# RWKV-6 linear attention and a star-ReLU MLP on one core: attention outputs transposed on TensorE to the end, one cumulative-sum product from chunk-batch 8, and a new hand-written order

## The chip, the cores and the metric

The program runs on one core of a Trainium2 chip. Its engines are TensorE (PE; its weight loads are a row of their own, PEld), VectorE (DVE), ScalarE (ACT), GpSimd (POOL) and SyncE (SP), which issues every DMA here. The metric is device microseconds of one execution, lower is better. An engine takes its instructions strictly in the order in which the program lists them, so an instruction that waits holds up everything behind it on its engine.

## The reference

Four batches, eight heads, 768 steps, 48 channels per head. The attention keeps a 48 x 48 state per head, and its output feeds an MLP with 3072 tokens, 384 inputs and 2048 hidden units.

```python
for t in range(S):
    cur = np.einsum('bhd,bhe->bhde', u[None] * kt, vt)
    y[:, :, t] = np.einsum('bhd,bhde->bhe', rt, state + cur)
    state = wt[:, :, :, None] * state + np.einsum('bhd,bhe->bhde', kt, vt)
...
x = np.ascontiguousarray(attn_out.transpose(0, 2, 1, 3)).reshape(B * S, H * D)
h = x @ w_in
r = np.maximum(h, 0.0)
g = s * (r * r) + b
return (g @ w_out).astype(np.float32)
```

## The kernel before

**Chunk-batches.** The 768 steps are cut into six chunks of 128, and with four batches this makes 24 chunk-batches, numbered n = 0 to 23. Chunk-batches 0 and 1 are two chunks of one batch that are handled as a packed pair; the last four (n = 20 to 23) need no new state. Two chunk-batches make one MLP tile T = 0 to 11 of 256 tokens.

**Attention steps of chunk-batch n**, with the names that the order uses:

- `load n.0` to `n.3` bring w, r, k, v (192 KB each; 384 KB for the pair 0 and 1). `ln` (ACT, line 316) takes log w.
- `cum` (PE) makes the cumulative sums over time: a strict one (line 386, tile `cums` half 0) and a negated inclusive one (line 390, half 1), one 128 x 384 product each, and four one-column products for the chunk's total decay (line 395). `exp` (ACT, lines 410 and 412) turns both halves, 768 columns, into factors `E`. `l2` (POOL) spreads the decay.
- The kernel has a second form of this, which is off: from chunk-batch `ONE` on, only the strict product is made and exponentiated, `inc` (DVE, line 422) adds log w to the strict sum in PSUM, and `exn` (ACT, line 432) takes the exponential of the negated sum. `ONE = 24` means never.
- `mul` (DVE, line 449) multiplies r and k by the factors. `tr` (PE) and `tev` (ACT) transpose the products for n below 9; from 9 on (`DTK`), `tev` is one DMA transpose (line 505).
- `mt` (PE, line 541) makes the 128 x 128 score tiles, `msk` (DVE, line 552) masks them, `dmm` (PE, line 636), `sup` (DVE) and `st` (POOL) update the state, `ymm` (PE, lines 595 and 604) makes the output, `rkp`, `rku`, `yd` (POOL) and `cd` (DVE) its u-term, `vb` the bf16 cast of v, and `yev` (DVE, line 649) the sum of both, `x_sb`.
- `x_sb` must be transposed for the MLP. For n below `DTX = 12`, `xtr` (PE, line 697) makes three 128 x 128 transposes into PSUM, and `xev` (ACT, line 712) copies them to `xT`. From 12 on, `xev` is a DMA transpose that SP issues (line 515), and there is no `xtr`.

**MLP steps of tile T.** `g1 T.i` (PE, line 746) makes hidden columns in eight parts of six 256-column products; `relu T.i` (ACT, line 759) evacuates each, 128 x 512, from PSUM; `sq T.i` squares it on ACT (line 769) or DVE (line 771). `g2 T.i` (PE, line 790) is the second product in parts of four 384-column products, `oev` (DVE, line 801) its evacuation, `store` the DMA out. `li`, `lo` load the two weights in four pieces of 768 KB, `ci`, `co` cast them. `g1` parts 0 and 1 need piece 0 of w_in, parts 2 and 3 piece 1, parts 4 and 5 piece 2, parts 6 and 7 piece 3.

**PSUM rings.** `cum` and `mt` share one buffer (ring A): each waits until the one before it has been evacuated. `tr`, `dmm`, `ymm` and `xtr` share two (ring B), `g1` has two (h), `g2` two (o).

**The order.** All of this is issued in one list written out by hand, `ORDER`. A word is a step; `@A`, `@D`, `@P` put it on ACT, DVE or POOL; `+5` means five idle 128 x 256 matmuls (line 1107) on PE. Without a suffix, a square goes to ACT where T is 2 or more and 8T + i is odd, otherwise to DVE. Where the order begins the first tile, before:

```
dmm0 mul2 +5 cum3
load4.0 exp3 sup0 +5 tr2 rkp3 st0 cd1 +1 mt1
```

Of the kernel before, what the change touches and what calls it, by code (L numbers as in the profile page):

```python
# [10 lines left out]
AF = mybir.ActivationFunctionType  # L11
# [12 lines left out]
VB = 6  # L24
PK = 2
PKD = 1.55
ONE = 24
DTK = 9
DTX = 12
DK2 = 24  # L30
DX2 = 24
SQE = 'DA'
# [3 lines left out]
SLACK = 0.2  # L36

ORDER = """
load0.0 load_u load0.2 load0.1 load2.0 load0.3 ln0 +15 u_mm ln1 load3.1 +1 cum0 exp0 load3.0 +5
cum1 l20 mul0 load2.1 exp1 rkp0 +1 tr0 load2.2 ln2 mul1 tev0 +6 cum2 load3.2 u_ev +2 tr1 exp2 rku0  # L40
li0 tev1 l21 cd0 rkp1 load3.3 vb1@A +14 mt0 vb0@A msk0 rku1 ln3 load2.3 +5 dmm0 mul2 +5 cum3
load4.0 exp3 sup0 +5 tr2 rkp3 st0 cd1 +1 mt1 tev2 yd0 msk1 li1 rkp2 ci0 li2 +13 ymm0 mul3 li3 mt2
l22 yev0 yd1 tr3 msk2 +1 ymm1 lo0 tev3 vb2 rku2 yev1 +2 xtr0 +1 mt3 xev0 rku3 xtr1 cd2 ln4 +1 dmm2
xev1 sup2 yd2 vb3@A cd3 +6 g10.0 ci1@A msk3 ymm2 l23 yd3 dmm3 g10.1 yev2 relu0.0 cum4 lo1 sup3
xtr2 relu0.1 g10.2 sq0.0 small2 sq0.1@A ci2@D dmm1 relu0.2 g10.3 load5.0 sup1 xev2 g10.4 sq0.2
relu0.3 ci3 ymm3 relu0.4 g10.5 yev3 load4.1 xtr3 relu0.5 g10.6 co0 xev3 g10.7 relu0.6 sq0.4
colsum0 load4.2 sq0.3@A g11.0 exp4 lo2 co1 g20.4 relu0.7 lo3 g20.0 l24 sq0.5 ln5 load4.3 colsum1
sq0.6 relu1.0 g20.5 sq0.7 g11.1 load6.0 g11.2 relu1.1 mul4 cum5 relu1.2 g11.3 rkp4 load5.1 exp5
g20.1 sq1.0@A co2 g11.4 relu1.3 tr4 sq1.1 relu1.4 load5.2 st3 g11.5 sq1.3@A colsum2 co3 relu1.5
load6.1 g20.2 tev4 g20.6 vb4 small rku4 colsum3 sq1.5@A mt4 cssplit load7.0 g20.7 msk4 l25 st1  # L50
csspread g20.3 load6.2 csevac sq1.2 dmm4 ln6 g11.6 mul5 load6.3 cum6 relu1.6 load5.3 rkp5 g11.7
oev0.1 exp6 load8.0 tr5 cd4 rku5 g21.4 oev0.0 ln7 load7.1 tev5 sup4 g21.5 yd4 st2 st4 ymm4 load7.2
relu1.7 mul6 cum7 g21.0 exp7 load7.3 rkp6 yev4 tr6 sq1.7@A mt5 load9.0 sq1.4 tev6 g21.1 l27 cd5
vb5 msk5 xtr4 ln8 rku6 load8.1 g21.2 xev4 dmm5 g21.6 vb6@A yd5 sup5 load8.2 sq1.6@A cum8 l26 ymm5
mul7 exp8 load9.1 dmm6 g21.3 rkp7 yev5 vb7@A g21.7 load10.1 sup6 xtr5 cd6 l28 mt6 rku7 xev5
load9.2 oev1.0 tr7 ln9 g12.0 msk6 tev7 st5 load8.3 g12.1 yd6 relu2.0 dmm7 cum9 load10.2 relu2.1
mul8 ymm6 exp9 g12.2 load10.0 rkp8 yev6 g12.3 relu2.2 sup7 mt7 load13.0 st6 relu2.3 tr8 msk7
sq2.2@A g12.4 rkp9 store0.0 tev8 g12.5 oev1.1 sq2.0@A ymm7 load11.0 sq2.1@D mt8 relu2.4 sq2.3@D
xtr6 cd7 g22.0 vb8@A load9.3 msk8 yd7 relu2.5 g12.6 ln10 load11.3 l29 g12.7 rku9 yev7 sq2.4@A
load12.0 g22.4 xev6 relu2.6 sq2.5@D dmm8 xtr7 st7 store0.1 relu2.7 g22.1 sup8 sq2.6@A cd9 rku8  # L60
g22.5 load10.3 xev7 cum10 ln11 mul9 g13.0 exp10 load11.1 g13.1 sq2.7 mul10 g22.2 load11.2 relu3.1
g22.6 tev9 l210 cd8 relu3.0 rkp10 ln12 ymm8 cum11 sq3.0@A yd9 g13.2 load13.1 exp11 yd8 g22.3 tev10
relu3.2 g13.3 rku10 oev2.0 cum12 relu3.3 load13.2 g13.4 sq3.2 vb9@A rkp11 yev8 g22.7 ln13 cd10
load12.1 sq3.1 g13.5 mul11 exp12 xtr8 dmm9 load12.2 oev2.1 g23.4 xev8 sup9 mt9 relu3.4 g23.0 st9
relu3.5 msk9 tev11 sq3.5 g13.6 st8 vb10@A g13.7 relu3.6 sq3.4 dmm10 l211 load12.3 ymm9 sq3.3 vb11
sup10 mt10 load13.3 rku11 relu3.7 yev9 g23.5 sq3.6@A msk10 xtr9 l212 store1.1 g23.1 rkp13 xev9
g23.6 sq3.7@D g14.0 yd10 load15.0 ymm10 relu4.0 mul12 dmm11 cum13 load14.0 g14.1 st10 yev10 exp13
cd11 g23.2 store1.0 rkp12 vb12@A xtr10 load14.1 mt11 relu4.1 g14.2 mul13 sq4.1 load14.2 sq4.0@A
g14.3 sup11 relu4.2 g23.3 msk11 st11 load14.3 sq4.2@A g14.4 tev12 yd11 ln14 g23.7 relu4.3 rku12
oev3.0 cum14 relu4.4 oev3.1 ymm11 load15.1 exp14 g14.5 l213 yev11 tev13 g14.6 sq4.3@D ln15 l214  # L70
relu4.5 sq4.4 cum15 rku13 xev10 load16.0 g14.7 exp15 mul14 xtr11 g24.4 relu4.6 load15.2 g24.0 l215
sq4.6@A sq4.5@D vb14 cd12 relu4.7 g24.5 load15.3 rkp14 xev11 dmm12 mt12 vb13@A g15.0 yd12 msk12
tev14 g15.1 relu5.0 g24.1 sup12 sq5.0@A sq4.7@D relu5.1 mt13 load17.0 ymm12 ln16 g15.2 yev12 dmm13
cd13 rkp15 g24.2 xev12 msk13 g15.3 yd13 store2.1 dmm14 g24.6 sup13 relu5.3 st12 store2.0 relu5.2
cum16 mul15 ymm13 sq5.1 load16.1 g24.3 exp16 rku15 sup14 g15.4 load16.2 vb15@A yev13 mt14 load18.0
rku14 relu5.4 cd15 g15.5 xev13 ln17 msk14 g24.7 sq5.3 st13 relu5.5 g15.6 load16.3 oev4.1 sq5.2@A
ymm14 cum17 tev15 dmm15 g25.4 exp17 mul16 g15.7 store3.1 l217 oev4.0 g25.5 load17.1 rkp16 ln18
cd14 sq5.5 g25.0 relu5.6 sq5.4 tev16 cum18 l216 sup15 relu5.7 yd14 g25.6 sq5.7 g16.0 st14 yev14
exp18 store3.0 g16.1 sq5.6 relu6.0 xev14 rku16 mt15 sq6.0@A g16.2 relu6.1 msk15 vb16 load17.2
g25.7 yd15 relu6.2 g16.3 st15 load19.0 ymm15 relu6.3 g25.1 load18.1 yev15 g16.4 sq6.3@D load17.3  # L80
oev5.1 g25.2 relu6.4 dmm16 xev15 sq6.2@A g16.5 sup16 sq6.1 g25.3 mul17 relu6.5 load18.2 mt16 rkp17
cd16 g26.0 ln19 tev17 msk16 g16.6 st16 g26.1 relu6.6 oev5.0 load19.1 cum19 sq6.6@A vb17 g26.4
store4.1 sq6.5 l218 yd16 sq6.4@A g26.5 load19.2 exp19 g17.0 rku17 g16.7 relu7.0 rkp18 load18.3
ymm16 relu6.7 g17.1 yev16 g17.2 store4.0 cd17 relu7.1 sq6.7@D xev16 mt17 mul18 relu7.2 dmm17 g26.2
sq7.1 sup17 load20.0 sq7.0@A g26.3 msk17 g17.3 rkp19 load20.1 g17.4 load19.3 oev6.0 yd17 ymm17
relu7.4 load20.2 g26.6 rku18 yev17 relu7.3 g26.7 tev18 sq7.2 g17.5 vb18 ln20 g27.0 sq7.4 l219
relu7.5 sq7.3@D xev17 g17.6 st17 oev6.1 sq7.5 g27.1 relu7.6 mul19 load21.0 dmm18 sq7.6@A cum20
g17.7 vb19 cd18 exp20 tev19 g27.4 rkp20 relu7.7 g27.5 sq7.7 mul20 load20.3 dmm19 g27.2 rku20 sup18
mt18 tev20 g18.0 msk18 rku19 g27.3 relu8.0 store5.1 sup19 yd18 g18.1 sq8.0@A cd19 load21.1 ymm18
cd20 relu8.1 yd19 g18.2 supn20 yev18 ln21 mt19 relu8.2 xev18 g18.3 msk19 yd20 g18.4 relu8.3  # L90
load21.2 g27.6 sq8.1@D relu8.4 store5.0 cum21 sq8.2@A ymm19 exp21 oev7.0 g18.5 load22.0 yev19
vb20@A g28.0 load23.0 sq8.3@D relu8.5 sq8.4 mt20 g18.6 sq8.5@D load22.1 msk20 g27.7 xev19 rkp21
g28.1 g28.2 load22.2 mul21 g18.7 ln22 load23.1 st19 oev7.1 ymm20 relu8.6 cum22 rku21 g28.4
load23.2 exp22 g28.5 st18 tev21 relu8.7 g28.6 ln23 sq8.7@D g19.0 sq8.6@A load21.3 g19.1 relu9.0
mul22 store6.0 cum23 relu9.1 g19.2 rkp22 yev20 exp23 tev22 g19.3 rku22 relu9.2 g28.7 relu9.3 g19.4
mul23 xev20 sq9.0@A g19.5 relu9.4 supn21 cd21 mt21 sq9.2@A store6.1 cd22 g19.6 sq9.1 load22.3
msk21 vb21 relu9.5 g28.3 rkp23 sq9.3 g19.7 oev8.0 relu9.6 tev23 yd21 ymm21 sq9.6@A g29.4 relu9.7
yev21 g29.5 sq9.5 sq9.4 mt22 xev21 g29.6 oev8.1 supn22 msk22 store8.0 g29.0 vb22@A yd22 load23.3
g29.1 sq9.7 rku23 ymm22 store7.0 g29.2 yev22 g29.3 store7.1 cd23 xev22 mt23 g110.0 msk23 g29.7
relu10.0 g110.1 supn23 vb23 g110.2 yd23 oev9.1 relu10.1 ymm23 store9.1 sq10.0 relu10.2 g110.3  # L100
sq10.1@D yev23 g110.4 relu10.3 oev9.0 xev23 g210.0 relu10.4 g210.4 sq10.4 store8.1 sq10.2 g110.5
sq10.3@D g110.6 relu10.5 g210.1 sq10.5@D relu10.6 g110.7 g210.2 relu10.7 g111.0 sq10.6@A g111.1
relu11.0 g210.5 sq11.0 relu11.1 sq10.7@D g111.2 g210.3 relu11.2 g111.3 oev10.0 g111.4 sq11.1@D
relu11.3 store10.0 store9.0 g211.0 sq11.3@D relu11.4 g111.5 sq11.4@A sq11.2@A g111.6 relu11.5
g210.6 relu11.6 g111.7 sq11.5 g210.7 relu11.7 g211.1 oev10.1 g211.2 sq11.7@D store10.1 sq11.6
g211.4 g211.8 g211.3 g211.5 oev11.0 g211.6 g211.9 store11.0 g211.7 g211.10 oev11.1 g211.11
store11.1 oev11.2 store11.2
"""

class Plan:  # L110

    def __init__(self, rings):
# [41 lines left out]
def kernel(  # L158
# [13 lines left out]
    nc = tc.nc  # L172

    B, H, S, D = r.shape
    L = 128
# [75 lines left out]
    xT = [None] * NT  # L251
# [455 lines left out]
    def xevac(n):  # L707
        c = cb[n]
        T, j = divmod(n, CPT)
        if j == 0:  # L710
            xT[T] = mlp.tile([128, KT, TOK], BF16, name="xT", tag="xT", bufs=XTB)
        nc.scalar.copy(out=xT[T][:, :, j * L : (j + 1) * L], in_=c["xt_ps"])


    def load_win(i):
# [21 lines left out]
    hs = {}  # L737
# [18 lines left out]

    def relu(T, i):
        rh = mlp.tile([128, FPQ, TOK], BF16, name="rh", tag="rh", bufs=4)
        nc.scalar.activation(out=rh, in_=hs[T, i], func=AF.Relu)  # L759
        hs[T, i] = rh  # L760

    def sq_eng(T, i):
# [385 lines left out]
```

## Time and profile before

| what | value |
|---|---|
| median of 13 runs | 191.34 us (188.84 to 192.5) |
| the profiled execution, time | 191.34 us |
| its span, first to last instruction | 189.5 us |
| outside the span | 1.84 us |
| PE busy | 182.7 us (96% of the span) |
| ACT busy | 134.3 us (71%) |
| DVE busy | 128.9 us (68%) |
| POOL busy | 104.6 us (55%) |
| granted TensorE clock | 1.00 |

Busy time counts an instruction from its start to its end. On PE a matmul overlaps the next one, so what a matmul costs in a dense stream is the distance from its start to the next start, not its duration: one `g1` part shows a duration of 0.82 us and the next one starts 0.65 us later. The same holds, less strongly, on DVE and ACT, where the end of one instruction overlaps the start of the next by about 0.1 us.

### The profile page before, as it was taken

To read this page: it belongs to the slowest core of one execution; us is meant where nothing else is said; L and a number is where in the kernel's file an instruction comes from. 1 tells how busy PE (TensorE), PEld (TensorE's weight loads), DVE (VectorE), ACT (ScalarE), POOL (GpSimd) and SP (SyncE) were. 2 spreads that over 40 slices of the span, in tenths; PEclk is the share of its full clock that TensorE was granted. 3 is DMA by queue.
4 is the path that set the end of the run, shared out by engine and by line. 5 is a ranking of instruction groups with operands and counts; after the bars stand their busy time and mean duration, and the time that the engine had idled before them with its cause. 6 is when DMAs were issued, how large, how long until landed. Compare 5 with 4: busy or idle time off the path is not lost.

```text
span 189.5 us, 5062 instructions
## 1 busy us (share of the span) xinstructions
PE 182.7 (96%) x1984; PEld 142.8 (75%) x1984; DVE 128.9 (68%) x214; ACT 134.3 (71%) x254; POOL 104.6 (55%) x138
## 2 busy tenths in 40 slices
PE   7999989999989999999999999999999999999992
PEld 5577868877659878877877877788787786788872
DVE  7368775757969964797959945478698668562241
ACT  3496696795969898959976896776685698157720
POOL 3667913227979659596558394837935575200000
PEclk9999999999999999999999999999999999999999
DMA  5999998998979899997997988889688897630212
GB/s 144 249 213 246 287 386 264 273 238 170 203 150 212 187 215 201 184 216 173 205 171 167 174 209 167 169 205 224 137 179 191 174 216 153 189 92 17 83 42 83
DMA packets 122601, 35.32 MB, mean 186 GB/s; under 512 B 117329, under 2 KB 120530, under 8 KB 122578
## 3 DMA queue, kind: packets, MB, share of 16 engines
q1 hardware_dynamic: 122578, 35.01, 82.3%
q8 instruction: 15, 0.25, 0.5%
q14 instruction: 8, 0.07, 0.1%
HBM read 25.17 MB, written 4.72 MB: 158 GB/s over the span
## 4 chain that ended last, share of the span: by engine, by line
PE 65%; SPq 17%; DMA 11%; issue 2%; ACT 1%; POOL 1%; DVE 1%; DVEq 0%; ACTq 0%
PE o_ps L790 27%; PE h_ps L746 27%; SPq L295 14%; DMA wi_st<-in_moe_w_in_dram 5%; DMA wt<-in_w_dram 3%; PE mt_ps L541 3%; DMA rkt<-in_k_dram 3%; PE y_ps L604 2%; PE y_ps L595 2%; SPq L303 1%; PE cums L386 1%; PE cums L390 1%; PE d_ps L636 1%; SPq L717 1%; POOL w_in L878 1%
## 5 line engine op out<-in xcount | busy, mean ns | idle before, releaser
L759 ACT ACTIVATE rh<-h_ps 128x512 bf16<-128x512 f32 x96 | 56.1, 597 | 28.3 <-PE h_ps L746 27.0
L746 PE MATMUL h_ps<-xT,w_in 128*128 128x256 bf16 x576 | 74.9, 273 | 0.9 <-ACT rh L759 0.6
L790 PE MATMUL o_ps<-w_out,gT 128*128 128x384 bf16 (+1 forms) x400 | 73.3, 320 | 0.0
L746 PEld LDWEIGHTS <-w_in 128*128 128x128 bf16 x576 | 60.8, 114 | 6.5 <-DVE w_in L880 0.9
L790 PEld LDWEIGHTS <-gT 128*128 128x128 bf16 x400 | 36.7, 98 | 16.7
L321 POOL TENSOR_TENSOR rkp<-rkt 128x384 f32<-128x384 f32 x22 | 27.3, 1242 | 16.8 <-DMA rkt<-in_k_dram 16.8
L769 ACT ACTIVATE gT<-rh 128x512 bf16<-128x512 bf16 x52 | 32.0, 628 | 0.5
L552 DVE TENSOR_TENSOR mt_sb<-mt_ps,tri_strict 128x1024 bf16<-128x1024 f32 x22 | 26.8, 1219 | 6.1 <-PE mt_ps L541 6.1
L449 DVE TENSOR_TENSOR prd<-rkt,E 128x768 bf16<-128x768 f32 x22 | 24.7, 1125 | 6.5 <-ACT E L410 3.5
L327 POOL TENSOR_TENSOR rku<-rkp,u_bc 128x384 f32<-128x384 f32 x24 | 25.6, 1072 | 2.1 <-DVE u_bc L903 1.8
L771 DVE TENSOR_TENSOR gT<-rh 128x512 bf16<-128x512 bf16 x44 | 20.2, 479 | 7.0 <-ACT rh L759 7.0
L410 ACT ACTIVATE E<-cums 128x768 f32<-128x768 f32 x24 | 19.5, 811 | 7.3 <-PE cums L378 2.8
L350 POOL TENSOR_TENSOR yd<-vt,cd 128x384 bf16<-128x384 f32 x22 | 18.3, 837 | 8.4 <-DVE cd L344 6.2
L801 DVE SCALAR_TENSOR_TENSOR o_sb<-o_ps,s_bc,bconst 128x384 f32<-128x384 f32 (+1 forms) x25 | 14.9, 597 | 11.4 <-PE o_ps L790 11.2
L649 DVE TENSOR_TENSOR x_sb<-y_ps,yd 128x384 bf16<-128x384 f32 x24 | 13.3, 553 | 11.6 <-PE y_ps L604 8.9
L686 POOL TENSOR_TENSOR st<-stmp,l 128x384 bf16<-128x384 bf16 x16 | 15.1, 947 | 3.8 <-DVE stmp L677 3.8
L1107 PE MATMUL warm_ps<-warm_sb 128*128 128x256 bf16 x84 | 13.6, 299 | 1.1 <-DVE warm_sb L1064 1.1
L316 ACT ACTIVATE logw<-wt 128x384 bf16<-128x384 f32 x22 | 11.6, 529 | 3.1 <-DMA wt<-in_w_dram 3.1
L344 DVE TENSOR_REDUCE cd<-rku 128x8 f32<-128x384 f32 x24 | 12.9, 542 | 1.2 <-POOL rku L327 1.2
L462 POOL TENSOR_TENSOR l<-E,par 128x8 f32<-128x8 f32 x20 | 6.8, 341 | 11.2 <-ACT E L412 11.2
L878 POOL CAST vb<-vt 128x384 bf16<-128x384 f32 x11 | 6.0, 544 | 11.2 <-DMA vt<-in_v_dram 7.2
L1107 PEld LDWEIGHTS <-warm_sb 128*128 128x128 bf16 x84 | 8.2, 106 | 3.4 <-DVE warm_sb L1064 1.0
(93 smaller groups left out, 176.6 us busy)
## 6 DMA issues: line engine op xcount, KB each, us to landing
out_dram<-o_sb SPq DMA_DIRECT2D x23, 192.0 KB, 2.4
wt<-in_w_dram SPq DMA_DIRECT2D x22, 192.0 KB, 4.2
rkt<-in_r_dram SPq DMA_DIRECT2D x22, 192.0 KB, 3.8
rkt<-in_k_dram SPq DMA_DIRECT2D x22, 192.0 KB, 3.8
vt<-in_v_dram SPq DMA_DIRECT2D x22, 192.0 KB, 3.6
wi_st<-in_moe_w_in_dram SPq DMA_DIRECT2D x4, 768.0 KB, 6.4
wo_st<-in_moe_w_out_dram SPq DMA_DIRECT2D x4, 768.0 KB, 7.8
pkt<-in_w_dram SPq DMA_DIRECT2D x1, 384.0 KB, 3.4
```

The lines of the kernel that those rows point to most:

```text
L295: nc.sync.dma_start(out=dst, in_=src[bb, :, t0 : t0 + L, :].transpose([1, 0, 2]))
L321: nc.gpsimd.tensor_tensor(out=rkp, in0=c["r"], in1=c["k"], op=ALU.mult)
L327: nc.gpsimd.tensor_tensor(out=rku.rearrange("t h d -> t (h d)"), in0=c["rkp"].rearrange("t h d -> t (h d)"), in1=u_bc, op=ALU.mult,)
L410: nc.scalar.activation(out=E[:, :, 0:HD], in_=ps[:, :, 0:HD], func=AF.Exp)
L449: nc.vector.tensor_tensor(out=prd[:, :, :, 0:D], in0=c["rk"], in1=c["E"][:, :, 0:HD].rearrange("t x (h d) -> t x h d", h=H), op=ALU.mult,)
L552: nc.vector.tensor_tensor(out=m.rearrange("s g p t -> s (g p) t"), in0=c["mt_ps"].rearrange("s g p t -> s (g p) t"), in1=(masks[n % 2] if ...
L746: nc.tensor.matmul(ps[:, f, :], lhsT=w_in_sb[ft // FPP][:, kt, :].rearrange("p (m j) -> p j m", j=FPP)[:, ft % FPP, :], rhs=xT[T][:, kt, : ...
L759: nc.scalar.activation(out=rh, in_=hs[T, i], func=AF.Relu)
L769: nc.scalar.activation(out=g, in_=rh, func=AF.Square)
L771: nc.vector.tensor_tensor(out=g, in0=rh, in1=rh, op=ALU.mult)
L790: nc.tensor.matmul(os_[T, k][:, cols], lhsT=gT[T][:, ft, tt * 128 : (tt + 1) * 128], rhs=w_out_sb[ft // FPP][:, ft % FPP, cols], start=(ft ...
L1107: nc.tensor.matmul(warm_ps, lhsT=warm_sb[:, 0:128], rhs=warm_sb, start=True, stop=True)
```

## The change

Three constants and functions change, and the whole order is written anew.

- `ONE` goes from 24 to 8: chunk-batches 8 to 23 make one cumulative sum on PE; `inc` and `exn` make the other.
- `DTX` goes from 12 to 24: chunk-batches 12 to 23 are transposed by `xtr` on PE, too, and no DMA transposes `x_sb`.
- `xevac` and `relu` may run on DVE where the order says `@D`.

Counted over the two orders: `relu` 96 on ACT before, now 69 on ACT and 27 on DVE; `sq` 52 on ACT and 44 on DVE before, now 66 and 30; `xev` 12 on ACT and 12 by DMA before, now 16 on ACT and 8 on DVE; `co` 4 on DVE before, now 2 on DVE and 2 on ACT; 16 `inc` and 16 `exn` are new; 84 idle matmuls become 76. Loads, stores, weights and the number of all other steps stay.

```diff
-ONE = 24
+ONE = 8
 DTK = 9
-DTX = 12
+DTX = 24
...
+load0.0 load0.2 load_u load0.1 load2.0 ln0 ln1 load2.1 +18 cum0 load2.2 u_mm exp0 load0.3 +2 cum1
+l20 mul0 li0 exp1 rkp0 +1 tr0 load3.0 ln2 mul1 tev0 load2.3 +6 cum2 u_ev +2 tr1 exp2 rkp2 load3.1
+tev1 mul2 vb0@A +14 mt0 rku0 vb1@A msk0 +5 dmm0 load3.2 rkp1 tr2 sup0 +1 mt1 tev2 li1 l22 rku1 cd0
+msk1 ci0 load3.3 rku2 st0 cd1 +15 ymm0 li2 yd0 ln3 cd2 vb2@A mt2 l21 yev0 yd1 lo0 msk2 +3 xtr0 +1
+ymm1 yd2 xev0 rkp3 cum3 yev1 dmm2 li3 exp3 sup2 +2 xtr1 +4 ymm2 xev1 small2 mul3 ci1@A +2 g10.0
+l23 yev2 tr3 vb3 relu0.0@D g10.1 rku3 tev3 load4.0 dmm3 g10.2 sup3 relu0.1 xtr2 ci2@D mt3 relu0.2
+g10.3 sq0.1@A cd3 lo1 dmm1 msk3 relu0.3 yd3 g10.4 co0@A g10.5 xev2@D sup1 ymm3 load4.1 sq0.2@A
+sq0.0 yev3 load5.0 g20.4 relu0.4 ci3 load4.2 xtr3 colsum0 xev3@D g20.0 ln4 relu0.5@D st1 sq0.3@A
+g10.6 lo2 g10.7 sq0.5 relu0.6 cum4 co1 relu0.7 lo3 g11.0 exp4 sq0.6 g11.1 load5.1 st2 sq0.4
...
+ln8 load6.3 g21.6 sup5 tev6 l27 cd6 l26 cum8 yd5 load10.0 ymm4 sq1.7@A inc8 ymm5 st5 yev4 exp8
+g21.2 load11.0 yev5 xtr4 mt6 mul7 xev4 xtr5 load8.1 g21.3 exn8 st4 msk6 xev5 tr7 vb7 ln9 load8.2
...
@@ xevac
-        nc.scalar.copy(out=xT[T][:, :, j * L : (j + 1) * L], in_=c["xt_ps"])
+        out = xT[T][:, :, j * L : (j + 1) * L]
+        if pl.ops["xev", n]["eng"] == "ACT":
+            nc.scalar.copy(out=out, in_=c["xt_ps"])
+        else:
+            nc.vector.tensor_copy(out=out, in_=c["xt_ps"])
@@ relu
-        nc.scalar.activation(out=rh, in_=hs[T, i], func=AF.Relu)
+        if pl.ops["relu", T, i]["eng"] == "ACT":
+            nc.scalar.activation(out=rh, in_=hs[T, i], func=AF.Relu)
+        else:
+            nc.vector.tensor_scalar_max(out=rh, in0=hs[T, i], scalar1=0.0)
```

## The prediction

> **What bounds the kernel now.** I read the windows first (where does an engine never rest?), then PE's timeline in those stretches, then the waits, then the start, where PE does rest. Windows by stage; columns are stretch, length, busy time and count of PE, PEld, DVE, ACT, POOL, clock, DMA share, GB/s:
>
> ```profile
> 0.00:23.00 23.00, 21.58 (x290) 15.74 (x291) 14.93 (x36) 13.76 (x24) 15.28 (x33) 1.00 0.90 224
> 31.00:57.00 26.00, 25.22 (x297) 19.20 (x298) 19.06 (x30) 20.07 (x40) 14.59 (x18) 1.00 0.89 202
> 57.00:97.00 40.00, 39.82 (x446) 32.52 (x444) 31.65 (x46) 35.23 (x73) 29.97 (x38) 1.00 1.01 201
> 97.00:137.00 40.00, 40.00 (x417) 30.85 (x416) 28.22 (x46) 28.92 (x56) 27.37 (x33) 1.00 0.91 177
> 137.00:186.00 49.00, 49.00 (x464) 38.85 (x462) 29.03 (x49) 30.00 (x54) 14.60 (x16) 1.00 0.57 134
> ```
>
> PE has no idle time from 57 to 186 us: whatever adds PE work there adds its full length, whatever holds PE adds the length of the hold, and nothing gives it back. The DMA and SP are busy there too, but PE does not wait for them. PE's timeline in a dense part (start, duration, what):
>
> ```profile
> 51.19 0.33 PE L697 MATMUL xt_ps<-identity,x_sb 128*128 128x128 bf16 x3
> 51.36 0.81 PE L790 MATMUL o_ps<-w_out,gT 128*128 128x384 bf16 x4
> 52.01 0.33 PE L636 MATMUL d_ps<-vb,prd 128*128 128x96 bf16 x4
> 52.18 0.81 PE L790 MATMUL o_ps<-w_out,gT 128*128 128x384 bf16 x4
> 52.83 0.33 PE L386 MATMUL cums<-logw,tri_strict 128*128 128x384 bf16 x1
> 52.99 0.33 PE L390 MATMUL cums<-logw,ntri_incl 128*128 128x384 bf16 x1
> 53.15 0.24 PE L395 MATMUL cums<-ones,logw 128*128 128x1 bf16 x4
> ```
>
> Prices are start-to-start distances: three transposes 0.17 us, one cumulative product 0.16 us, a `g2` part 0.65 us. With such distances for every step I lay the written order out as PE work: 166.8 us without the idle matmuls (both MLP products 125 of it). The span of 189.5 is then 166.8 plus 22.7 of lag. Lag at a step is its start minus the PE work ahead of it: 13.5 at the first `g1` (23.26 - 9.8), 15.0 at `g1 0.6` (30.90 - 15.9), 16.8 near 64 us, 19.2 at the last matmul's end, and 3.5 for the last evacuation and store. Where the lag grows early, PE's timeline, DVE's and the chain of waits say why:
>
> ```profile
> 28.50 0.85 PE L746 MATMUL h_ps<-xT,w_in 128*128 128x256 bf16 x6 [0.64 <-ACT rh L759]
> 30.90 1.28 PE L746 MATMUL h_ps<-xT,w_in 128*128 128x256 bf16 x10 [0.28 <-POOL w_in L878]
> 55.91 0.34 PE L697 MATMUL xt_ps<-identity,x_sb 128*128 128x128 bf16 x3 [0.65 <-DVE x_sb L649]
> ```
>
> ```profile
> 27.48 0.96 DVE L880 CAST w_in<-wi_st 128x1536 bf16<-128x1536 f32 x1 [1.25 <-DMA wi_st<-in_moe_w_in_dram]
> 54.43 0.96 DVE L449 TENSOR_TENSOR prd<-rkt,E 128x768 bf16<-128x768 f32 x1 [1.49 <-ACT E L412]
> ```
>
> ```profile
> 18.95 10.37 DMA wi_st<-in_moe_w_in_dram
> 29.38 1.47 POOL w_in L878
> 49.05 5.26 DMA rkt<-in_k_dram
> ```
>
> `g1 0.4` starts as the cast of w_in piece 2 ends (27.48 + 0.96 = 28.44), although the wait names ACT; `g1 0.6` waits for piece 3, which lands at 29.3; `xtr5` waits for `yev5`, which stands on DVE behind `mul7`, which waits for k of chunk-batch 7 until 54.3 (the wait names ACT, but the chain the DMA). So the weights and the early loads set the start, PE the rest.
>
> **The change, part by part.**
>
> *PE work.* Sixteen products go: 16 x 0.16 = -2.6 us. Twelve `xtr` of three transposes come: 12 x 0.17 = +2.0. Net -0.6. Here a rule speaks against the change: the Trainium skill, "TensorE: Matmul & The Clock Gate", section "Back-to-back issue gap", says that 128-column matmuls in a stream of weight load and matmul sustain about 81 ns each, since both set the spacing. Then 36 transposes cost an estimated 2.9 us and the change adds 0.3. The row shows 0.17 / 3 = 57 ns in just such a stream, so I take -0.6 and keep +0.3 as the other end.
>
> *Idle matmuls.* 84 become 76, 8 x 0.11 = 0.9 us of filler. They stand before the first `g1`, where PE waits anyway: zero. Without that cover, -0.9.
>
> *ACT.* Away: 27 `relu` x 0.597 = 16.1 us. New: 14 `sq` x 0.628 = 8.8, two `co` x 1.48 = 3.0 (row of w_in on ACT), 4 `xev` x 0.479 = 1.9, one `vb` less, -0.5 (POOL gets it, 0.544, with 45% idle). The split exponential: before, one 768-column row of 0.811; after, a 384-column one (near the 0.479 copy from PSUM) and `exn` (near the 0.516 cast from SBUF), +0.18, less the small row of 0.172 that is joined to the first one in 12 of 16: +0.9. Sum -2, so ACT stays near 132 of its 134 us.
>
> *DVE.* New: 16 `inc`, two operands, one in PSUM, as `yev`: x 0.553 = 8.8. 27 `relu` of 512 columns from PSUM: between the rows of 384 (553 ns) and 1024 (1219 ns), 1.04 ns a column, so 0.686 x 27 = 18.5. A rule promises much less: "ScalarE: Activation LUTs", section "Rules for kernel authors", wants relu on VectorE, up to three times faster per element in bf16. By it 27 x 0.2 = 5.4 us. But this relu reads fp32 from PSUM, and both PSUM rows run at 1.04 ns, above ACT's 597 ns for the same tile; I take 18.5. 8 `xev`: 0.553 by the same rows, 0.35 if 16-bit PSUM data went at double rate; 4.4. Away: 14 `sq` x 0.479 = 6.7 and two `co` x 0.96 = 1.9. Sum +23: DVE goes from 129 to about 152 us, 80% of the span. It is dense where PE work 36 to 72 is done: I count 55 DVE instructions there, 38.7 us by their rows, against 42 and 30.9 before. Back to back they overlap (0.55-us rows start every 0.47 us), so 55 x 0.08 = 4.4 comes off: 34.3 us of DVE in 36 of PE. It fits, with 5% to spare. I cost it at nothing; the cover is that spare.
>
> *New waits on PE.* `xtr12` to `xtr23` wait for `yev`, and everything behind them on PE with them, then hold a ring-B buffer until `xev`. In the order at least 1.47 us of PE work lies between `ymm` and its `xtr` there; needed are 0.55 plus two hand-overs (`yev5` ends at 55.85, `xtr5` starts at 55.91). `xtr21` has 0.98 us before the `g1` that reads it, needing about 0.7. `cum` now frees ring A after both `exp` and `inc`; at least 1.47 us of PE work follow. `mul` comes later, since `inc` then `exn` (1.07) replace the one `exp` (0.81). All covered unless DVE's queue is late. No DMA transpose of `x_sb`: 12 x 1.2 us of SP's queue and 12 x 98 KB go; the loads and stores behind them go out earlier, but from 57 us PE waits for no load, so zero (between zero and the 2 us by which the lag grows after 67 us, most of it 0.1-us gaps at each `mt`).
>
> *The start.* Before, `cum3` stood between `msk0` and `mt1` on the single ring-A buffer, so `mt1` waited for `exp3` until 16.55 us; now `mt1` follows `msk0`, which ended at 14.6. `mt1`, `ymm0`, `xtr0` and `xtr1` move up by about two, and `g1 0.0` comes at about 21.2 in place of 23.26. But DMA is full there (share 0.9 to 1.0), and bytes decide: w_in piece 3 is now issued behind w_out piece 0, 6912 KB into the list in place of 6336, so it lands at about 30.7 in place of 29.3 and is cast by 32.2. The order puts 17.0 us of PE work before `g1 0.6` in place of 15.9: lag 32.2 - 17.0 = 15.2 against 15.0. The two microseconds are lost again, late weights take their place. Later, k of 7 comes 192 KB earlier in the list (about 1.2 us), and `mul7` stands behind `yev5`: the hole of 0.65 at `xtr5` and what followed it shrink. From both I take -0.7 at 57 us, between +0.5 and -1.9 (the whole head start).
>
> *Sum.* -0.6 - 0.7 = -1.3 on the profiled execution of 191.34, which equals the median: 190.0 us.
>
> **The rivals.** A: as above; 190.0, own range 187.9 to 191.0.
>
> B: slower, by DVE's queue. The 34.3 us hold only if DVE idles no more than 1.7 us in that stretch; before, it idles 8.4 of 40 between 57 and 97 us, waiting for PE, ACT and DMA. With 10% idle the stretch takes 34.3 / 0.9 = 38.1, +2.1 us, and about 0.9 more in the less dense rest; PE stops at ring h (`relu`), ring A (`inc`) or ring B (`xev`). Less 0.6 of PE work: 193.7; with half of that, 192.5. For it: PE has no slack that would absorb a hold. Against it: DVE's longest waits today are for PE (11.2 us on `o_ps`, 8.9 on `y_ps`, 6.1 on `mt_ps` by the list of waits): it idles because it is early, and such idle time can be filled.
>
> C: the change does nothing that lasts: the start gives nothing or loses 0.5, and transposes cost what the products save: 191.2, between 190.2 and 192.3.
>
> **How the numbers follow.** A change of 0.5%, 0.96 us, is about what a measurement of this kernel can tell from none. A has 0.50, of which 0.10 lies within 0.5%; B 0.29, all slower; C 0.21: 0.04 faster, 0.10 the same, 0.07 slower. Faster 0.44, same 0.20, slower 0.36. Likeliest is A, 190.0; alone it would be 187.9 to 191.0. The range runs from A's low end to 194.3, which leaves out the worst of B.
>
> **What would show it.** Right: PE idle under 0.5 us after 60 us, one 384-column product per chunk-batch from 8 on, transposes at 0.17 us per three, the first `g1` near 21 us with PE holes before `g2 0.4` or `g1 0.6` behind weight casts, DVE near 150 us busy, its relu near 0.69 us. Wrong: PE idle on `rh`, `inc` or `xT` of DVE between 60 and 130 us (B); first `g1` not before 23 us (C); transposes at 80 ns, or a lag below 15.5 at 64 us, which would make the gain larger than mine.

## The result, and the profile after

| | before | after |
|---|---|---|
| median of the runs | 191.66 us (48 runs, 188.84 to 193.57) | 188.69 us (11 runs, 187.41 to 191.04) |
| ratio of the times | | 0.9882, 95% interval 0.985 to 0.9913 |
| profiled execution, time | 191.34 us | 187.45 us |
| its span | 189.5 us | 185.6 us |
| PE, DVE, ACT, POOL busy | 182.7, 128.9, 134.3, 104.6 us | 180.2, 149.7, 131.8, 106.8 us |

By the ratio the change makes the kernel 1.2% faster, 2.3 us; by the medians of all runs it is 3.0 us. (The ratio compares the runs within 1.5% of each kernel's fastest, which leaves out the slower part of the wide spread of before; the medians alone would give 0.9845.) The two profiled executions differ by 3.9 us: that of after is one of its fastest, that of before lies at its median. A second profile of after, taken later (189.45 us, span 187.6), is one of its slowest. Both are used below, so that what differs between them is not put down to the change.

Windows of the kernel after, by stage (stretch, length, busy time and count of PE, PEld, DVE, ACT, POOL, clock, DMA share, GB/s):

```profile
0.00:23.00 23.00, 21.59 (x293) 15.94 (x294) 16.82 (x38) 14.19 (x24) 16.23 (x34) 1.00 0.95 257
31.00:57.00 26.00, 26.00 (x315) 20.56 (x312) 20.98 (x35) 23.52 (x44) 15.09 (x21) 1.00 0.97 219
57.00:97.00 40.00, 39.85 (x438) 31.80 (x437) 37.47 (x57) 33.34 (x68) 31.63 (x37) 1.00 1.02 195
97.00:137.00 40.00, 39.97 (x436) 31.27 (x434) 36.10 (x55) 28.47 (x58) 27.99 (x34) 1.00 0.96 189
```

PE is as full from 57 us on as it was, and now also from 31 to 57 us (26.00 of 26.00, before 25.22). DVE is busy 37.47 of 40 us in its densest stretch, and PE has no hole for it: its list of waits has three entries, all before 28 us. The first 23 us show what else is new: DMA moves 257 GB/s there in place of 224.

A dense part of PE's timeline after (start, duration, what):

```profile
50.57 0.33 PE L700 MATMUL xt_ps<-identity,x_sb 128*128 128x128 bf16 x3
51.16 0.34 PE L700 MATMUL xt_ps<-identity,x_sb 128*128 128x128 bf16 x3
51.34 0.81 PE L800 MATMUL o_ps<-w_out,gT 128*128 128x384 bf16 x4
51.99 0.61 PE L478 MATMUL trps<-identity,prd 128*128 128x128 bf16 x8
53.27 0.33 PE L389 MATMUL cums<-logw,tri_strict 128*128 128x384 bf16 x1
53.43 0.24 PE L398 MATMUL cums<-ones,logw 128*128 128x1 bf16 x4
```

Three transposes take 51.34 - 51.16 = 0.18 us, and one cumulative product (0.16 us) now stands where two did. Groups of the page of after:

```profile
L767 ACT ACTIVATE rh<-h_ps 128x512 bf16<-128x512 f32 x69 | 40.6, 596 | 22.7 <-PE h_ps L753 19.3
L769 DVE TENSOR_SCALAR rh<-h_ps 128x512 bf16<-128x512 f32 x27 | 18.2, 685 | 5.0 <-PE h_ps L753 4.1
L425 DVE TENSOR_TENSOR inc<-cums,logw 128x384 f32<-128x384 f32 x16 | 8.8, 552 | 3.4 <-ACT E L420 1.1
```

Relu takes 685 ns on DVE and 596 on ACT. Where the time went is seen in the lag, the start of a step less the PE work ahead of it, counted in each kernel's own order (us):

| kernel | start of the first `g1` | lag there | at `g1 0.6` | at `g2 1.1` | at `g1 2.0` | at the last `g2` | span |
|---|---|---|---|---|---|---|---|
| before | 23.26 | 13.5 | 15.4 | 16.6 | 17.3 | 19.7 | 189.5 |
| after | 21.58 | 12.3 | 13.0 | 13.2 | 13.7 | 16.2 | 185.6 |
| after, second profile | 22.41 | 13.2 | 15.0 | 15.2 | 15.7 | 18.2 | 187.6 |

From `g2 1.1` on, the lag grows by 3.1 us before and by 3.0 after: nothing was won or lost there but PE work, of which there is 0.5 to 0.6 less. The rest of the gain is in place by then: 3.4 us in the one profile, 1.4 in the other.

### The profile page after: what moved, and what is told of

The parts are those of the page before. It is cut to its first block, busy times and chain, and to the rows that moved or that the text cites. A ratio compares the mean times of both kernels' runs of the same rounds, so it can differ in the third digit from the quotient of the medians.

```text
span 185.6 us, 5076 instructions
## 1 busy us (share of the span) xinstructions
PE 180.2 (97%) x1996; PEld 142.3 (77%) x1996; DVE 149.7 (81%) x249; ACT 131.8 (71%) x250; POOL 106.8 (58%) x139
## 4 chain that ended last, share of the span: by engine, by line
PE 86%; DVE 4%; issue 2%; ACT 2%; DVEq 0%; ACTq 0%
PE o_ps L800 32%; PE h_ps L753 31%; PE mt_ps L544 4%; PE warm_ps L1117 3%; PE y_ps L607 2%; PE xt_ps L700 2%; PE cums L389 2%; PE y_ps L598 2%; PE trps L478 2%; PE d_ps L639 2%; DVE prd L452 1%; PE cums L398 1%; PE y_ps L587 1%; DVE mt_sb L555 1%; PE cs_ps L839 1%
## 5 line engine op out<-in xcount | busy, mean ns | idle before, releaser
L767 ACT ACTIVATE rh<-h_ps 128x512 bf16<-128x512 f32 x69 | 40.6, 596 | 22.7 <-PE h_ps L753 19.3
L800 PEld LDWEIGHTS <-gT 128*128 128x128 bf16 x400 | 36.2, 98 | 16.4 <-DVE gT L781 0.3
L779 ACT ACTIVATE gT<-rh 128x512 bf16<-128x512 bf16 x66 | 40.4, 628 | 1.8 <-DVE rh L769 1.5
L452 DVE TENSOR_TENSOR prd<-rkt,E 128x768 bf16<-128x768 f32 x22 | 27.0, 1229 | 1.6 <-ACT E L435 0.6
L353 POOL TENSOR_TENSOR yd<-vt,cd 128x384 bf16<-128x384 f32 x22 | 20.7, 945 | 11.5 <-DVE cd L347 11.5
L769 DVE TENSOR_SCALAR rh<-h_ps 128x512 bf16<-128x512 f32 x27 | 18.2, 685 | 5.0 <-PE h_ps L753 4.1
L689 POOL TENSOR_TENSOR st<-stmp,l 128x384 bf16<-128x384 bf16 x16 | 13.2, 828 | 9.5 <-DVE stmp L680 9.5
L781 DVE TENSOR_TENSOR gT<-rh 128x512 bf16<-128x512 bf16 x30 | 14.8, 507 | 2.4 <-ACT rh L767 2.4
L1117 PE MATMUL warm_ps<-warm_sb 128*128 128x256 bf16 x76 | 12.1, 301 | 1.1 <-DVE warm_sb L1074 1.1
L347 DVE TENSOR_REDUCE cd<-rku 128x8 f32<-128x384 f32 x24 | 12.9, 542 | 0.0
L717 ACT COPY xT<-xt_ps 128x384 bf16<-128x384 bf16 x16 | 7.6, 476 | 6.1 <-PE xt_ps L700 6.1
L425 DVE TENSOR_TENSOR inc<-cums,logw 128x384 f32<-128x384 f32 x16 | 8.8, 552 | 3.4 <-ACT E L420 1.1
```

The lines of the kernel that those rows point to most:

```text
L353: nc.gpsimd.tensor_tensor(out=yd, in0=c["v"], in1=c["cd"].unsqueeze(2).to_broadcast([128, H, D]), op=ALU.mult,)
L452: nc.vector.tensor_tensor(out=prd[:, :, :, 0:D], in0=c["rk"], in1=c["E"][:, :, 0:HD].rearrange("t x (h d) -> t x h d", h=H), op=ALU.mult,)
L769: nc.vector.tensor_scalar_max(out=rh, in0=hs[T, i], scalar1=0.0)
L779: nc.scalar.activation(out=g, in_=rh, func=AF.Square)
L781: nc.vector.tensor_tensor(out=g, in0=rh, in1=rh, op=ALU.mult)
L800: nc.tensor.matmul(os_[T, k][:, cols], lhsT=gT[T][:, ft, tt * 128 : (tt + 1) * 128], rhs=w_out_sb[ft // FPP][:, ft % FPP, cols], start=(ft ...
```

## The experiments

Two theories stood at first: S, that the gain lies in the order of the start (up to `g1 2.0`), and R, that it lies in the rest (one product per chunk-batch, DVE's relu, no DMA transposes). All ratios are to the kernel before, run beside it on the same chip. The kernel after stands at 0.9882 and, repeated, at 0.9852.

**The start alone (e1_start).**

```diff
-ONE = 8
-DTX = 24
+ONE = 24
+DTX = 12
 ORDER: the words of after up to g1 2.0, without inc and exn,
        then the remaining words in the sequence of before
```

> The new order up to the first part of tile 2, then everything that is left in the old order's sequence, with two products and DMA transposes as before. Theory S (the gain lies in the start: at tile 2 PE stands 3.6 us further on, and nothing is gained or lost later but 0.6 us of PE work): span about 186.1, 3.4 us below before, ratio near 0.982, first g1 at 21.6 us. Rival R (the gain comes from what follows tile 2: fewer DMA transposes and a free SP queue, and the earlier start is lost again): span 189, ratio 0.997 to 1.0.

Measured: 189.76 us, ratio 0.9976 (0.9935 to 1.0017), span 188.2. The lag is 13.5 at `g1 0.6` and 13.8 at `g2 1.1`, 2.8 less than before: the start does what S says. But then PE stands idle for 1.4 us at one place. PE's and ACT's timelines of this kernel:

```profile
54.53 0.33 PE L634 MATMUL d_ps<-vb,prd 128*128 128x96 bf16 x4 [1.36 <-ACT vb L881]
```

```profile
53.97 0.51 ACT L881 CAST vb<-vt 128x384 bf16<-128x384 f32 x1 [0.96 <-DMA vt<-in_v_dram]
```

PE waits for the cast of a v that lands at 53.95 us: a load of the seam, where the old sequence goes on behind the new one. So S holds for the start itself, while the time of this kernel, 1.1 us below before by the medians, cannot be told from none.

**The rest alone (e2_rest).**

```diff
-ONE = 24
-DTX = 12
+ONE = 9
+DTX = 24
 ORDER: the words of before up to g1 2.0,
        then the remaining words in the sequence of after
```

> The old order up to the first part of tile 2, then everything that is left in the new order's sequence, one product from chunk-batch 9 and TensorE transposes to the end. Theory S: only the PE work is saved, 15 x 0.16 - 12 x 0.17 = 0.4 us, span 189.1, ratio 0.998. Rival R: span near 186 and ratio near 0.982.

Measured: 190.79 us, ratio 1.0012 (0.9965 to 1.0059). The rest alone gives no gain that can be seen, as S expected. Neither half carries the whole gain by itself.

**Two products again (e3_two_products).**

```diff
-ONE = 8
+ONE = 24
 ORDER: after, without its 16 inc and 16 exn
```

> The changed kernel with two products and one wide exponential again (no inc, no exn); all else in place. If the PE price of 0.16 us holds: 16 x 0.16 = +2.6 us, span 188.2, ratio to before near 0.995. If the product was hidden or cheaper in the stream (the rule's numbers), +1 to +1.8. DVE loses 8.8 us of work; if that load held PE somewhere, less than +2.

Measured: 190.63 us, ratio 1.0029 (0.9996 to 1.0062), span 188.2. PE work is 2.6 us more by the order. The ratio is 1.5% above that of after, 2.8 us, the median 1.9 us (0.4 of it outside the span), and the span 2.6 us above that of the first profile, with much the same lag at the last `g2` (16.4, there 16.2). Beside that profile PE work on this path counts in full; by the medians, more than half of it does.

**DMA transposes again (e4_dma_x).**

```diff
-DTX = 24
+DTX = 12
 ORDER: after, for n >= 12 xev (now a DMA) where xtr stood
```

> The changed kernel with DMA transposes of x_sb from chunk-batch 12 again, each in the place of its xtr in the order. PE work falls by 12 x 0.17 = 2.0 us. If nothing waits: span 183.6, ratio 0.978. But a DMA transpose took 1.2 us to issue and 2.7 us to land before, and the order leaves 0.98 us of PE work between xtr21 and its g1 and 1.09 at 13: those g1 would wait 2 to 3 us each, seven more leave about 2 us: +5 to +10 us in all, span 188 to 194.

Measured: 197.03 us, ratio 1.0325 (1.0257 to 1.0393), although PE has 2.0 us less to do. Its list of waits:

```profile
PE h_ps L750 <- DMA xT<-x_sb: 8.2, 5, 2.9
```

Five `g1` wait 8.2 us for a transposed x. By the DMA issues of before, such a transpose lands 2.7 us after its issue; `xtr` and `xev` need 0.17 and 0.48. The order of after leaves no room for the difference, so this is the price of DMA transposes in this order, not in one made for them.

**Relu and xT on ACT throughout (e5_act).**

```diff
 ORDER: after, with "@D" taken off 27 relu and 8 xev
```

> After, with all relu and all xT evacuations on ScalarE (27 relu and 8 xev less on VectorE). ScalarE gets 27 x 0.596 + 8 x 0.45 = 20 us more, 152 of 186 us (82%); VectorE falls by 21 to 128 us (69%). If the engine of these copies doesn't matter as long as neither is full: 188.7 us, ratio 0.988. If the choice of VectorE at those places is what keeps PE free (relu late on a full ScalarE queue, PE held at ring h): 2 to 5 us more, 191 to 194 us, ratio 1.0 to 1.015, with PE waits on rh of ScalarE.

Measured: 189.67 us, ratio 1.0005 (0.9969 to 1.0041), span 187.7: ACT 147.1 us busy, DVE 130.1. The intervals do not meet, so DVE's share is worth 1.0 us (by the medians) to 2.4 us (by the ratios, 1.0005 - 0.9882). PE's list of waits has only 0.3 us on ACT's relu; beside the first profile of after the lag is 0.8 us larger at `g1 0.6` and 1.6 larger at `g1 3.0`, in holes too short to be listed, while the span, 187.7, is that of the second profile (187.6). So the cost rests on the times of the runs; that it comes from the queue behind which a relu stands is likely, not shown. ACT is not full in any case.

Now the start itself. Two causes were possible: the sequence of SP's loads (L), and the place of `cum3` on ring A (C).

**Old loads in after (e8_old_loads).**

The loads alone, in their order among themselves:

```diff
-load0.0 load0.2 load_u load0.1 load2.0 load2.1 load2.2 load0.3 li0 load3.0 load2.3 load3.1 load3.2
-li1 load3.3 li2 lo0 li3 small2 load4.0 lo1 load4.1 load5.0 load4.2
+load0.0 load_u load0.2 load0.1 load2.0 load0.3 load3.1 load3.0 load2.1 load2.2 load3.2 li0 load3.3
+load2.3 load4.0 li1 li2 li3 lo0 lo1 small2 load5.0 load4.1 load4.2
```

> After, with the first 24 loads that SP issues in the sequence of before (the compute order is untouched). Theory L (the sequence of the loads brought the early start): first product near 22 to 23 us, weight casts before g1 0.4 and g1 0.6 late again, lag at g1 0.6 near 15.3 in place of 13.0, time 190.9 us, ratio 0.998 or a little above. Theory C (the place of cum3 on ring A brought it): first product stays near 21.6 us, lag at g1 0.6 below 13.7, time about 188.9 us, ratio 0.988.

Measured: 191.57 us, ratio 1.01 (1.0055 to 1.0145). The first `g1` starts at 25.09, the lag at `g1 0.6` is 16.9. ACT's timeline of this kernel, and that of after at the same step:

```profile
17.36 1.47 ACT L884 CAST w_in<-wi_st 128x1536 bf16<-128x1536 f32 x1 [1.29 <-DMA wi_st<-in_moe_w_in_dram]
```

```profile
15.45 1.48 ACT L886 CAST w_in<-wi_st 128x1536 bf16<-128x1536 f32 x1
```

Piece 0 of w_in lands at 17.34 us here and at 13.24 in after. The cast stands on ACT ahead of the casts of v, the evacuations of x and `exp3`, which all move back with it. PE's clock reads 0.71 from 20 to 24 us here, behind an idle stretch of 1.4 us; but three runs of this kernel whose clock was 0.997 or more took 191.16 to 191.66 us too, so the clock is not the cause.

**The old place of cum3 in after (e9_old_cum3).**

```diff
-dmm0 ... ln3 ... l21 ... rkp3 cum3 yev1 dmm2 li3 exp3
+ln3 l21 dmm0 cum3 exp3 ... rkp3 yev1 dmm2 li3
```

> After, with ln3, l2 3, cum3 and exp3 back ahead of mt1, where before has them. Theory C: mt1 waits for exp3 to free ring A, first product 2 us later at about 23.5 us, lag at g1 0.6 near 15, time 190.7 us, ratio 0.998. Theory L: the weights are there when they are needed, and the hold is refilled only partly from waiting PE time, so at most 1 us is lost: 189.0 to 189.7 us, ratio 0.988 to 0.991.

Measured: 190.42 us, ratio 1.002 (0.9984 to 1.0056). PE's timeline:

```profile
15.11 0.34 PE L387 MATMUL cums<-logw,tri_strict 128*128 128x384 bf16 x1 [0.31 <-DVE mt_sb L553]
16.70 0.42 PE L531 MATMUL mt_ps<-RK 48*64 48x128 bf16 x16 [0.43 <-ACT E L413]
```

`mt1` waits for `exp3` to give ring A back and starts at 16.70 (14.54 and 15.37 in the two profiles of after); the first `g1` comes at 23.61, 2.0 and 1.2 us later than there, and the span is 188.7, 3.1 and 1.1 us more. The second is the fairer pair: PE's opening ran at half pace in it and in e9 (see the end). By the ratios the old place costs 2.6 us. So C holds too, and theory L's "at most 1 us" falls: each of the two is needed.

**New loads in before (e7_loads)**, the reverse of e8.

> Before, with the first 24 loads that SP issues in the sequence of after. Theory L: w_in pieces land near 13, 21, 24 and 28 us as in after, no weight wait before g1 0.6, lag there near 13.5 in place of 15.4, time 2 us below before, ratio 0.990. Theory C: mt1 is still held by exp3 until 16.5 us, first product near 23.3 us, and the lag at g1 0.6 stays at 14 or above, time within 1 us of before, ratio 0.995 to 1.0. If the start needs both, half of the gain.

Measured: 196.17 us, ratio 1.0349 (1.0298 to 1.04), so it hit neither. The pieces land at 12.9, 21.9, 24.4 and 28.1 us, yet the first `g1` starts at 29.90. ACT's and PE's timelines:

```profile
28.96 0.52 ACT L314 ACTIVATE logw<-wt 128x384 bf16<-128x384 f32 x1 [3.26 <-DMA wt<-in_w_dram]
29.39 0.46 ACT L710 COPY xT<-xt_ps 128x384 bf16<-128x384 bf16 x1
```

```profile
29.90 1.05 PE L744 MATMUL h_ps<-xT,w_in 128*128 128x256 bf16 x6 [3.07 <-ACT xT L710]
```

In the old compute order `ln4` stands on ACT ahead of `xev1`. The new sequence fetches w of chunk-batch 4 five places later (it lands at 28.94 in place of 20.01), so ACT stands 3.26 us at `ln4`, with `xev1` and PE behind it. The kernel after has `ln4` behind `g2 0.0`. That is only half of the delay at the first `g1`: `mt1` starts at 19.95 already, 3.4 us later than in before. The new sequence fetches u one place later, PE stands idle for 0.98 us for it in the opening, and runs at half pace until 13.3 us.

**cum3 moved in before (e6_cum3).**

```diff
-dmm0 cum3 exp3 ... mul3 ... tr3 ... tev3 ... mt3
+dmm0 ... ymm1 cum3 exp3 ... xtr1 mul3 ... g10.0 tr3 tev3 ... g10.1 mt3
```

> Before, with cum3 and exp3 moved behind ymm1 (mul3, tr3, tev3, mt3, msk3 moved to match); loads as before. If the place of cum3 alone gives the head start and the late weights take it back (the prediction's step): first product near 22 us in place of 23.3, but piece 3 of w_in still lands near 29.3 us, so the lag at g1 0.6 stays at 15.0 to 15.4 and the time within 0.5 us of before, ratio 0.997 to 1.0. If the hold by cum3 alone was worth the gain: lag at g1 0.6 near 13, ratio 0.987.

Measured: 194.26 us, ratio 1.0146 (1.009 to 1.0202), slower by 2.7 us. Two things are seen. First, `exp3` now stands ahead of `xev0` on ACT and waits there for `cum3`, which waits for ring A behind `mt2`:

```profile
24.22 0.81 ACT L408 ACTIVATE E<-cums 128x768 f32<-128x768 f32 x1 [2.97 <-issue]
24.98 0.49 ACT L710 COPY xT<-xt_ps 128x384 bf16<-128x384 bf16 x1
```

(after has `xev0` at 18.71, ahead of `exp3` at 20.28). Second, PE runs at half pace in the profiled execution until about 12 us (more of this at the end); in e2, with the same opening, such a pace alone makes the first `g1` 2.0 us late. So what the move of `cum3` costs by itself stays open here.

**Both in before (e10_both)**: e6_cum3 with the loads of e7_loads.

> The kernel above, with the first 24 loads in the sequence of after as well. If the two together, and nothing else of the new start, carry the gain: w_in pieces land near 13, 21, 24 and 28 us, first product near 21.6 us, lag at g1 0.6 below 13.8, time 2.5 us below before, ratio 0.987. If the casts, copies and evacuations between have to be ordered to match as well: SP and ScalarE hold each other as with the loads alone (first product near 30 us there), and the time is above before.

Measured: 201.98 us, ratio 1.0555 (1.05 to 1.0611). The first `g1` starts at 29.30 behind the same `ln4` (ACT idle 2.68 us), and PE, idle for 2.56 us before it, falls to half speed. Windows of this kernel:

```profile
24.00:28.00 4.00, 2.15 (x26) 1.60 (x25) 2.54 (x5) 1.25 (x3) 1.68 (x4) 1.00 0.77 219
28.00:32.00 4.00, 2.61 (x22) 2.13 (x22) 0.00 (x0) 1.67 (x4) 1.96 (x2) 0.63 0.27 35
32.00:36.00 4.00, 2.30 (x18) 1.48 (x18) 0.96 (x1) 3.72 (x5) 0.00 (x0) 0.50 1.07 296
36.00:40.00 4.00, 3.69 (x26) 2.43 (x26) 2.79 (x6) 0.97 (x2) 0.00 (x0) 0.50 0.84 241
```

The lag grows from 20.3 at the first `g1` to 27.9 at `g1 0.6`. The two edits that are both needed in after are not enough in before. `ln4` does harm there, and so does an opening at half pace until 12.0 us; how much is due to each is not separated.

**After again, and a try at a better start (a0_after, e11_ymm1).**

> The changed kernel once more, unchanged, as the yardstick on this chip for the next one: 188.7 us, ratio 0.988.

```diff
-ymm0 li2 yd0 ln3 cd2 vb2@A mt2 l21 yev0 yd1 lo0 msk2 +3 xtr0 +1 ymm1 yd2 xev0 rkp3 cum3 yev1
-dmm2 li3 exp3 sup2 +2 xtr1 +4 ymm2 xev1
+ymm0 ymm1 li2 yd0 ln3 cd2 vb2@A mt2 l21 yev0 yd1 yev1 lo0 msk2 +3 xtr0 +1 yd2 xev0 rkp3
+dmm2 li3 sup2 +2 xtr1 cum3 +4 ymm2 xev1 exp3
...
-ci3
+ci3@D
```

> After, with ymm1 and yev1 directly behind ymm0 and yev0, cum3 and exp3 behind xtr1 and xev1, and w_in piece 3 cast on VectorE. From the trace of after: yev1 could end at 19.2 in place of 20.4, xev1 at 20.0 in place of 21.5, first product at 20.2 in place of 21.6. Piece 3 lands at 28.05 whatever is done; its cast on VectorE takes 0.96 in place of 1.46, so g1 0.6 could start at 29.1 in place of 29.7. If the weights limit from there on, 0.3 to 0.6 us less than after (188.2 us, ratio 0.986); if nothing is late, 1 us or more less; if VectorE or ScalarE is now late (yev1 ahead of msk2, exp3 behind xev1), 0 to 1 us more.

Measured: after 188.52 us, ratio 0.9852 (0.98 to 0.9903); e11 189.05 us, ratio 0.9893 (0.9855 to 0.9932). The try gains nothing. Its first `g1` starts at 22.45 (22.41 in the second profile of after): `xtr1` is done earlier, but PE goes on in its order, and `cum3`, idle matmuls and `ymm2` still stand ahead of the product.

The second profile of after shows why two executions of one kernel part by 2.0 us up to the first `g2` (29.88 and 27.91), 0.8 of it at the first `g1`. Timelines of POOL, DVE and PE there, and then the same steps in the first profile:

```profile
28.07 1.46 POOL L888 CAST w_in<-wi_st 128x1536 bf16<-128x1536 f32 x1 [0.68 <-DMA wi_st<-in_moe_w_in_dram]
28.26 1.55 DVE L781 TENSOR_TENSOR gT<-rh 128x512 bf16<-128x512 bf16 x1
29.88 0.50 PE L800 MATMUL o_ps<-w_out,gT 128*128 128x384 bf16 x2 [1.37 <-ACT logw L319]
```

```profile
27.43 0.42 DVE L781 TENSOR_TENSOR gT<-rh 128x512 bf16<-128x512 bf16 x1
27.91 0.82 PE L800 MATMUL o_ps<-w_out,gT 128*128 128x384 bf16 x4 [0.23 <-DVE gT L781]
28.11 1.46 POOL L888 CAST w_in<-wi_st 128x1536 bf16<-128x1536 f32 x1 [1.54 <-DMA wi_st<-in_moe_w_in_dram]
```

The square of `rh` on DVE takes 0.42 us, and 1.55 when it starts just after POOL's cast of piece 3: it ends 0.28 us after the cast. PE's wait names ACT, but it ends with that square (29.81). In the first profile the square came 0.7 us ahead of the cast. The Trainium skill, "SBUF — State Buffer", section "SBUF: two separate sides", describes this: POOL and a DVE instruction with two inputs in SBUF share a pair of ports, the first to start holds it for its whole instruction, and the other waits. The numbers agree. What decides which comes first is not the load, since piece 3 lands at 28.02 and at 28.05, but PE's pace in the opening. Timelines of PE, the first profile and then the second:

```profile
5.49 0.32 PE L374 MATMUL cums<-logw,hi_neg 128*128 128x384 bf16 x1
5.65 0.33 PE L374 MATMUL cums<-logw,hs_neg 128*128 128x384 bf16 x1
```

```profile
5.61 0.52 PE L374 MATMUL cums<-logw,hi_neg 128*128 128x384 bf16 x1
5.93 0.52 PE L374 MATMUL cums<-logw,hs_neg 128*128 128x384 bf16 x1
```

The cumulative products begin at 4.92 us in both, but run 0.32 us apart in the second in place of 0.16. The exponential behind them starts 0.49 us later (6.79, in the first 6.30), and `mt1` and the square 0.83 us later.

## Why the prediction was right, and where it was wrong

The direction and the path were right, at 190.0 us for a measured 188.69. By its steps:

- *PE work, -0.6: right.* By its times e3 puts the sixteen products at 1.9 to 2.8 us, for 2.6 by the order, and three transposes take 0.17 to 0.18 us. The 81 ns of the Trainium skill, "TensorE: Matmul & The Clock Gate", section "Back-to-back issue gap", do not hold for this stream.
- *ACT -2, DVE +23: right in kind.* ACT fell by 2.5 us and DVE rose by 20.8. Relu on DVE took 685 ns where 686 was taken, longer than the 596 on ACT. The copy of xT from PSUM took 0.35 us, the lower of the two bounds, not the 0.553 that was chosen; 8 of them explain 1.6 of the 2.2 us.
- *New waits on PE, none: right.* PE has no hole over 0.2 us after 57 us, so rival B, DVE's queue as the bound, did not come about at 81% of DVE's time.
- *DMA transposes gone, zero: consistent.* The lag grows as before from `g2 1.1` on. e4 prices only their return in the new order.
- *DVE or ACT for relu, nothing: wrong.* The prediction counted the move of 27 relu and 8 xev as busy time alone. e5 puts it at 1.0 to 2.4 us in the new order, by the times of the runs.
- *The start, -0.7: the mis-sized term.* It measured -3.4 us in the one profile and -1.4 in the other at `g2 1.1`; by the medians it is about 3.0 - 0.6 = 2.4, by the ratio 2.3 - 0.6 = 1.7, with what DVE's relu brings in it. The head start at `mt1` was seen rightly (first `g1` predicted at 21.2, found at 21.58 and 22.41), and e9 puts it at 1.2 to 2.0 us. (The lag of before at `g1 0.6`, 15.0 in the prediction, is 15.4 counted by the order.) What failed is "bytes decide": with w_in piece 3 behind 576 KB more, it was to land at 30.7 and take the head start back. It landed at 28.05 in the first profile of after and at 28.02 in the second; pieces 1 and 2 landed at 20.7 and 23.6 in place of 23.8 and 27.5.

The bytes were right, the rate was not. Before, the 6336 KB up to and with piece 3 had landed by 29.3 us, 216 KB per us. After, it was 6912 KB by 28.05, 246 KB per us. In the trace SP is seen to let them go sooner. DMA issues on SP's queue, before and then after:

```profile
15.00 2.63 SPq L295 DMA_DIRECT2D wt<-in_w_dram  x1
17.68 1.77 SPq L717 DMA_DIRECT2D wi_st<-in_moe_w_in_dram  x3
19.57 6.08 SPq L727 DMA_DIRECT2D wo_st<-in_moe_w_out_dram  x2
```

```profile
13.95 1.58 SPq L724 DMA_DIRECT2D wi_st<-in_moe_w_in_dram  x1
16.73 0.55 SPq L734 DMA_DIRECT2D wo_st<-in_moe_w_out_dram  x1
17.40 0.38 SPq L724 DMA_DIRECT2D wi_st<-in_moe_w_in_dram  x1
22.92 1.94 SPq L734 DMA_DIRECT2D wo_st<-in_moe_w_out_dram  x1
```

Before, piece 1 of w_in waits behind the w of chunk-batch 4 and goes out at 17.68; after, at 13.95. Piece 3 goes out at 17.40 in place of 18.95 (the third issue in the row of 17.68), and from there takes much the same, 10.6 and 10.4 us. Before, the issue of the second w_out piece holds SP until 25.3 us, since the stages of w_in come free only with their casts; after, these casts are done 2.4 us earlier and that piece goes out at 22.92, so the queue runs less dry (DMA share 0.95 in the first 23 us in place of 0.90). It is the sequence of the loads that does most of this, not the faster start: in e7, whose first `g1` comes only at 29.90, the pieces land at 21.9, 24.4 and 28.1 us, and in e9 piece 3 at 28.07. The compute order has a smaller part: in e8, with the old sequence, pieces 1 and 2 land at 22.7 and 25.1. The prediction added the new bytes to a landing time of the old trace, and the new sequence had moved the timetable. It had named the sign of its error: "a lag below 15.5 at 64 us, which would make the gain larger than mine". The lag there is 14.0 and 16.0 in the two profiles of after.

That the gain does not come apart is shown by e3, e5, e8 and e9: each takes one thing out of after, and by the ratios each costs as much as the whole gain or more (by the medians e5 costs a third of it). They sum to far more than the 3 us that separate the two kernels. e6, e7 and e10, which put one or two things into before, make it slower, but their openings also ran at half pace. What stays open is how much of the median's 3 us is the pace of PE in the first microseconds, since the profiles of one kernel differ by 2 us; what is known of it stands at the end.

## What to carry to other kernels

With queues that run strictly in order, do not price a moved load against the landing times of the old trace: work out when its issue is released (which cast frees its stage, what stands ahead of it on the issuing queue), then when it lands, then who waits. Where an order was fitted as a whole, pieces of it cannot be tried alone in another order; what a piece costs is learnt by taking it out of the order that has it, and such costs don't add. Before laying one or two microseconds at an edit's door, profile the same kernel twice.

## What was unexpected of the hardware

PE's pace. In before, the first cumulative products run 0.16 us apart; in the profiled execution of e6, whose order is the same up to there, 0.32. Timelines of PE, before and then e6:

```profile
6.01 0.33 PE L371 MATMUL cums<-logw,hi_neg 128*128 128x384 bf16 x1
6.18 0.33 PE L371 MATMUL cums<-logw,hs_neg 128*128 128x384 bf16 x1
```

```profile
6.76 0.53 PE L369 MATMUL cums<-logw,hi_neg 128*128 128x384 bf16 x1
7.08 0.53 PE L369 MATMUL cums<-logw,hs_neg 128*128 128x384 bf16 x1
```

The half pace lasts until 10 to 12 us in e2 and e6, which both have the opening of before; in e2, whose order is that of before up to `g1 2.0`, the first `g1` starts at 25.26 in place of 23.26. The clock row shows 1.00 through it, since a trace's first record of the clock is that of the full rate. These records agree with the distances: in the three profiles with the opening of before they stand at 5.1 us (before), 9.6 (e2) and 12.0 (e6), with the loads of after in it at 13.3 (e7) and 12.0 (e10). In the nine with the opening of after, where 18 idle matmuls in place of 15 and no wait for u stand ahead of `cum0`, they stand at 3.9 to 7.1. The Trainium skill, "TensorE: Matmul & The Clock Gate", section "Part 1: The HAM clock gate", has the array at half rate until it was busy for a window of some 3.4 us, and the window runs freely; that fits an opening that sometimes misses it.

So the steadier opening is a rival for a part of the gain. In e2 the 2.0 us at the first `g1` have shrunk to 0.55 at `g1 0.6` (31.45, in before 30.90), so most of it was made up there, where before waits for a weight cast; whether before loses time so in many of its runs was not tried, and this part of the idle matmuls' price, set at zero in the prediction, stays open. In e10 an idle stretch of 2.56 us, after two short ones, was enough to bring the half rate back until about 42 us.
